# Linear attention into two mixture stages: the matmuls of an attention iteration in another order, and three buffers for the raw weights

## The chip, the cores and the metric

The program runs on one core of a Trainium2 chip. The metric is the device time of one execution in microseconds (us), lower being better; the kernel before took 762.11 us in the median of three runs (761.12 to 762.54). The core has a matrix engine (TensorE, PE in the rows, with PEld for its weight loads), VectorE (DVE), ScalarE (ACT), GpSimd (POOL) and SyncE (SP). Each works through its own instructions in order. SP issues nearly all DMAs, POOL the indirect ones.

## The reference

Three stages follow each other. The first is gated linear attention over 4 batches, 8 heads, 768 steps and head size 48; the second sends each of the 3072 tokens to the best of 8 experts; the third multiplies two projections elementwise and applies two more matrices, which come as 64-bit floats.

```python
f = 1 / (1 + exp(-f_logit))
for t in range(S):                                   # attention, per batch and head
    state = f[t][:, None] * state + outer(k[t], v[t])
    y[t] = q[t] @ state
x = y.transpose(0, 2, 1, 3).reshape(3072, 384)
...
logits = (x / (norm(x) + 1e-6)) @ (emb / (norm(emb) + 1e-6)).T / tau
e = argmax(logits, 1)                                # expert of each token
gate = softmax(logits)[range(N), e]
x = gate[:, None] * (relu(x @ w1[e]) @ w2[e])        # per token's expert
...
a, b = x @ g1, x @ g2                                # g1, g2, g3, go: 64-bit inputs
out = ((a * b) @ g3) @ go
```

## The kernel before

The kernel has three stretches. In the first, 24 units of attention (4 batches by 6 chunks of 128 steps, all heads of a chunk at once) go through a loop of 26 iterations, software-pipelined: iteration i works on unit i for one part, on unit i-1 for the next, and so on to i-4. The table `parts` (L685) sets the order of the parts, each with how many units it lags; every engine gets its instructions in that order, and the program's order is kept. In the second stretch each expert's tokens are fetched, multiplied by w1 and w2 (`g1_step`, L824, and `g2_step`, L838), and written to a dense buffer; in the third the two projections and the output follow (L921 and L934).

The parts of one iteration, with the tile that each writes: `s_gate` turns the gates of unit i (ft, L343) and makes their sigmoid on ACT (L351, L352); `s_qk` turns q and k of unit i-1 (qt, kt, L343) and scales them on DVE (qd and kd, L371 and L373); `s_scan` makes the running products on DVE (L357, L359); `s_score` multiplies kd by qd for unit i-2 (a, L382), and ACT and POOL copy and mask the result (am, L384 and L385); `s_kb` turns kd (kb, L394); `s_uu` makes the state's increment of unit i-3 from kk and v (uu, L424), which `s_state` adds on DVE (L433), `s_sm` scales on POOL (L440) and `s_blocks` copies on ACT (sbd, L448); `s_out` makes the outputs of unit i-3, first from the state (y, L405), then from am and v (y, L408); `s_xt` turns them to token rows and makes the logits (xl, L454), which ACT copies (xt, L455) and DVE sums (lg, L464). There are eight accumulator banks, given out in turn, so that a matmul also waits until the tile of eight allocations before has been read.

The matmuls use the 128 by 128 array in three ways. ft, qt, kt, kb, xl and the y of L405 use all rows and columns; a works on 64 rows at a time (64\*128 in the rows of the profile); uu and the y of L408 write 64 columns at a time (128\*64). Below, such a way is called an array mode.

Beside the attention, three things run in the loop. `route` (L494) ranks finished units by expert in groups of four: some 20 small DVE instructions, a power on POOL (L510), a few matmuls (rk) and one indirect DMA a unit (L556) that scatters its tokens to the scratch xsd. It is a generator; `turn` advances it by one step four times an iteration (twice that in the last two). `conversions` (L197) turns the 64-bit weights to 32 bits a piece at a time: a DMA of the raw piece (L207), two ACT instructions (L223, L224), two on DVE (L226, L227), one add on POOL (L230); `convert` and `bg.pull` advance it from iteration 5 on. In the first stretch it makes 16 pieces, in the second 20 more. At the end of an iteration SP loads the gates, k, q and v of later units (L333), the next raw piece and, in iterations 2 to 9, zeros for part of xsd (L718).

After the loop the last units are routed (`pre`, three units, and `last`, one), the counts of the experts are ranked (`finish_route`, L565), and the first expert's tokens are read back (xs, L783). PE fills this time with products of the two last matrices (wpb, L184).

Of the kernel before, what the change touches and what calls it, by code (L numbers as in the profile page):

```python
# [19 lines left out]
def attn_moe_glu_kernel(  # L20
# [21 lines left out]
    P = 128  # L42
# [65 lines left out]
    GAP_TILES, ZF, BG0, BGP = 4, 2, 5, 2  # L108
# [88 lines left out]
    def conversions(pieces):  # L197
        raws = {}

        def load_raw(i):  # L200
            if i < len(pieces):
                loads.append(lambda: fetch_raw(i))

        def fetch_raw(i):
            src, n, _, _ = pieces[i]
            raws[i] = cv.tile([P, 512, 2], I32, name="raw", bufs=2)[:, 0:n, :]
            SP.dma_start(out=raws[i], in_=src.bitcast(I32).rearrange("p (n w) -> p n w", w=2))  # L207

        load_raw(0)
        load_raw(1)  # L210
        for i, (_, n, tag, put) in enumerate(pieces):
# [164 lines left out]
    def s_score(u):  # L376
        qd, kd = st["qd", u], st["kd", u]
        m = wk.tile([P, 2, NP, P], F32, name="am")
        a = [bank([P, NP, P], "a") for _ in range(2)]
        for j in range(NP):  # L380
            for hb in range(2):
                PE.matmul(out=a[hb][:, j, :], lhsT=kd[64 * hb:64 * hb + 64, j, :], rhs=qd[64 * hb:64 * hb + 64, j, :])  # L382
        for hb in range(2):
# [14 lines left out]

    def s_out(u):
        b, c = units[u]  # L400
        am, qd = st.pop(("am", u)), st.pop(("qd", u))
        vv = vs[u % NV]
        y = bank([P, NP, P], "y")
        for j in range(NP if c else 0):
            PE.matmul(out=y[:, j, :], lhsT=sbd[b][:, j, :], rhs=qd[:, j, :], start=(j == 0), stop=False, skip_group_check=True)  # L405
# [64 lines left out]
    def make_en():  # L470
        et = rt.tile([E, DM], F32, name="et")
        s = rt.tile([E, 6], F32, name="es")
        ep = rt.tile([E, H, 64], F32, name="ep")
# [20 lines left out]
    def route(u0, n):  # L494
# [6 lines left out]
        t8 = lambda name: rt.tile([P, 4, E], F32, name=name, bufs=2)[:, 0:n, :]  # L501
        t1 = lambda name, dt=F32: rt.tile([P, 4], dt, name=name, bufs=2)[:, 0:n]
        mx, m2, m, d = t1("mx"), t1("m2"), t8("m"), t8("d")
        r0, r1, rinv = t1("r0"), t1("r1"), t1("rinv")
        nb = rt.tile([P, E], F32, name="nb", bufs=2)
        sq = ssq[:, us]
        t, sm = t8("t"), t1("sm")
        pos, pi = t1("pos"), rt.tile([P, 4], I32, name="pi", bufs=2)[:, 0:n]
        flat = lambda a: a.rearrange("p g e -> p (g e)")
        G.tensor_tensor(out=r0, in0=sq, in1=half[:, 0:1].to_broadcast([P, n]), op=ALU.pow)  # L510
# [4 lines left out]
        V.tensor_tensor(out=d, in0=L, in1=wide(mx), op=ALU.subtract)  # L515
# [12 lines left out]
        V.tensor_scalar(out=r1, in0=r1, scalar1=0.5, scalar2=1e-6, op0=ALU.mult, op1=ALU.add)  # L528
# [4 lines left out]
        PE.matmul(out=flat(rk), lhsT=tri, rhs=flat(O), start=True, stop=False, skip_group_check=True)  # L533
# [4 lines left out]
        V.reciprocal(out=rinv, in_=r1)  # L538
# [559 lines left out]
```

## Time and profile before

| | us |
|---|---|
| median of three runs | 762.11 |
| the profiled execution: its whole time | 760.98 |
| its span, first to last instruction | 759.3 |
| PE busy | 732.8 (97%) |
| DVE, ACT, POOL busy | 362.8, 355.7, 361.1 |

The span begins with the first instruction and ends with the last; the whole time of that execution has 1.7 us more around it. Matmuls are pipelined, so that a busy PE row can still hold gaps between starts: the starts of successive groups tell how long a group kept PE. PEclk is the share of TensorE's full clock that was granted. Unless a row says otherwise, times are us from the start of the span.

### The profile page before, as it was taken

How to read it: one execution, taken by the hardware profiler on the slowest of the kernel's cores; microseconds unless marked ns; L12 is line 12 of the kernel's file. 1: busy time of each engine (PE TensorE's matmuls, PEld its weight loads, DVE VectorE, ACT ScalarE, POOL GpSimd, SP SyncE). 2: the span in 40 equal slices, each digit the busy share in tenths (PEclk: the TensorE clock that was granted, in tenths of full speed). 3: DMA queues.
4: the chain of work that ended last, by engine and by line, in shares of the span. 5: the costliest groups of instructions: out<-in, count | busy, mean ns of one | idle time of the engine just before them, and what ended most of it. 6: DMA issues, size and time to landing. Idle time of an engine off the chain costs nothing.

```text
span 759.3 us, 12752 instructions
## 1 busy us (share of the span) xinstructions
PE 732.8 (97%) x4825; PEld 666.6 (88%) x4825; DVE 362.8 (48%) x716; ACT 355.7 (47%) x723; POOL 361.1 (48%) x412
## 2 busy tenths in 40 slices
PE   6999899999899998999999999999999999999996
PEld 6888788788799998999999998888888888888885
DVE  8888799995646544543542323232222322323222
ACT  5899687884555646645554542212112112121220
POOL 4567778886497766756555681221112202211102
PEclk9999999999999999999999999999999999999999
DMA  9999978822576797646433340010010100100101
GB/s 184 246 243 247 244 180 210 216 56 94 186 255 209 228 254 228 209 132 203 146 115 123 126 126 1 0 42 1 1 41 1 43 0 1 42 1 2 41 1 45
DMA packets 132653, 89.64 MB, mean 118 GB/s; under 512 B 106465, under 2 KB 114665, under 8 KB 132585
## 3 DMA queue, kind: packets, MB, share of 16 engines
q1 hardware_dynamic: 129513, 79.29, 38.3%
q0 software_dynamic: 3072, 9.46, 3.4%
q8 instruction: 40, 0.66, 0.4%
q14 instruction: 28, 0.23, 0.1%
HBM read 70.57 MB, written 18.17 MB: 117 GB/s over the span
## 4 chain that ended last, share of the span: by engine, by line
PE 68%; issue 10%; DVE 8%; DMA 5%; POOL 4%; ACT 3%; SPq 0%; POOLq 0%; DVEq 0%; ACTq 0%
PE acc L838 12%; PE hb L824 11%; PE pa L921 10%; PE pb L921 10%; PE ob L934 10%; DMA stg<-in_moe_w_dram 3%; PE wpb L184 2%; PE a L382 2%; PE y L408 2%; DVE sf L357 2%; PE xl L454 2%; DVE w L359 1%; PE ft L343 1%; POOL xsd L556 1%; PE y L405 1%
## 5 line engine op out<-in xcount | busy, mean ns | idle before, releaser
L133 POOL TENSOR_TENSOR wl<-stg,wh 128x384 fp32r<-128x384 f32 (+1 forms) x121 | 139.0, 1172 | 67.6 <-ACT wh L132 59.1
L924 DVE TENSOR_TENSOR a<-a,pb 128x512 f32<-128x512 f32 x48 | 33.0, 688 | 181.5 <-PE pb L921 175.7
L934 PE MATMUL ob<-wp,ab 128*128 128x384 f32 x576 | 108.2, 339 | 0.0
L838 PE MATMUL acc<-h,wh 128*128 128x448 f32 (+7 forms) x384 | 104.3, 351 | 3.1 <-ACT h L826 2.2
L934 PEld LDWEIGHTS ob<-wp,ab 128*128 128x128 f32 x576 | 102.3, 188 | 3.7
L824 PE MATMUL hb<-xT,wh 128*128 128x448 f32 (+7 forms) x384 | 102.6, 348 | 0.0
L827 DVE SCALAR_TENSOR_TENSOR h<-hb,h 128x448 fp32r<-128x448 f32 (+7 forms) x64 | 37.1, 580 | 111.6 <-ACT h L826 111.5
L921 PE MATMUL pa<-x,wh 128*128 128x512 f32 x288 | 90.2, 394 | 0.0
L921 PE MATMUL pb<-x,wh 128*128 128x512 f32 x288 | 89.9, 393 | 0.0
L941 POOL DMA_INDIRECT out_dram<-o,didx x24 | 23.2, 968 | 129.8 <-DVE o L940 126.4
L923 ACT COPY a<-pa 128x512 f32<-128x512 f32 x48 | 28.2, 587 | 120.6 <-PE pa L921 120.6
L132 ACT CAST wh<-stg 128x384 fp32r<-128x384 f32 (+1 forms) x124 | 64.4, 566 | 39.6 <-DMA stg<-in_moe_w_dram 34.6
L133 POOL TENSOR_TENSOR x<-xd,x 128x512 fp32r<-128x512 f32 x18 | 22.8, 1292 | 121.4 <-ACT x L132 121.4
L926 ACT CAST ab<-a 128x512 fp32r<-128x512 f32 x48 | 29.8, 621 | 104.8 <-DVE a L924 104.8
L838 PEld LDWEIGHTS acc<-h,wh 128*128 128x128 f32 x384 | 70.4, 188 | 6.6 <-ACT h L826 3.2
L824 PEld LDWEIGHTS hb<-xT,wh 128*128 128x128 f32 x384 | 70.8, 188 | 1.4
L824 PE MATMUL hb<-xT,wl 128*128 128x448 f32 (+7 forms) x192 | 66.7, 348 | 0.0
L838 PE MATMUL acc<-h,wl 128*128 128x448 f32 (+7 forms) x192 | 66.7, 347 | 0.0
L921 PEld LDWEIGHTS pb<-x,wh 128*128 128x128 f32 x288 | 54.2, 188 | 12.7
L385 POOL TENSOR_SCALAR_AFFINE_SELECT am<-am 128x512 f32<-128x512 f32 x48 | 51.7, 1098 | 23.1 <-ACT am L384 23.1
L921 PEld LDWEIGHTS pa<-x,wh 128*128 128x128 f32 x288 | 53.6, 188 | 9.2
L826 ACT ACTIVATE h<-hb 128x448 fp32r<-128x448 f32 (+7 forms) x64 | 32.5, 508 | 61.3 <-PE hb L824 61.0
(184 smaller groups left out, 1363.8 us busy)
## 6 DMA issues: line engine op xcount, KB each, us to landing
stg<-in_moe_w_dram SPq DMA_DIRECT2D x32, 768.0 KB, 5.1
raw<-in_moe_w_dram SPq DMA_DIRECT2D x28, 512.0 KB, 4.2
xsd<-wp SPq DMA_DIRECT2D x8, 675.5 KB, 5.8
xs<-xsd SPq DMA_DIRECT2D x8, 675.5 KB
f<-in_f_logit_dram SPq DMA_DIRECT2D x24, 192.0 KB, 3.9
k<-in_k_dram SPq DMA_DIRECT2D x24, 192.0 KB, 4.4
q<-in_q_dram SPq DMA_DIRECT2D x24, 192.0 KB, 4.6
v<-in_v_dram SPq DMA_DIRECT2D x24, 192.0 KB, 4.3
```

The lines of the kernel that those rows point to most:

```text
L132: A.copy(out=hi, in_=src)
L133: eng.tensor_tensor(out=lo, in0=src, in1=f32(hi), op=ALU.subtract)
L385: G.affine_select(out=m[:, hb], in_=m[:, hb], pattern=[[0, NP], [1, P]], compare_op=ALU.is_ge, fill=0.0, base=0, channel_multiplier=-1)
L824: PE.matmul(out=b, lhsT=w[x][:, kk, cs], rhs=xT[e][y][:, kk, :], start=(kk + n == 0), stop=(kk == KD - 1 and n == 2))
L826: A.activation(out=h[0], in_=b, func=AF.Relu)
L827: V.scalar_tensor_tensor(out=h[1], in0=b, scalar=0.0, in1=f32(h[0]), op0=ALU.max, op1=ALU.subtract)
L838: PE.matmul(out=acc[d], lhsT=w[x][:, s % 4, d * P:(d + 1) * P], rhs=hs[s][y], start=(s + n == 0), stop=(s == KF - 1 and n == 2))
L921: PE.matmul(out=b, lhsT=w[x][:, kk, cs], rhs=x2[n][y][:, kk, :], start=(kk + m == 0), stop=(kk == KD - 1 and m == 2))
L923: A.copy(out=t, in_=pa)
L924: V.tensor_tensor(out=t, in0=t, in1=pb, op=ALU.mult)
L926: A.copy(out=ab[s][0], in_=t)
L934: PE.matmul(out=oacc[t], lhsT=ab[s][x][:, t * P:(t + 1) * P], rhs=wp[:, y, s, :], start=(s + m == 0), stop=(s == KF - 1 and m == 2))
```

## The change

The parts of an iteration are put in another order, and two of them are cut in two: `s_score` keeps the matmuls and leaves the copies and masks to `s_mask`, and the product with the state moves from `s_out` to `s_inter`. The raw weights get three buffers; the tile z goes, and its values overwrite the low words in the raw tile. A raw buffer is thereby free after the add on POOL, no longer after the second DVE instruction, and the next load is asked for there. `route` takes groups of six, makes the square root's correction without the extra step, ranks with fewer and wider matmuls, writes the position as an integer at once, and copies the ids on POOL. The zeros are written in iterations 2, 3, 5, 6, 7, 9, 10 and 11. Two small tiles of the start reuse others.

```diff
-    GAP_TILES, ZF, BG0, BGP = 4, 2, 5, 2
+    GAP_TILES, BG0, BGP, RAW = 4, 5, 2, 3
+    FILL = (2, 3, 5, 6, 7, 9, 10, 11)
...
-            raws[i] = cv.tile([P, 512, 2], I32, name="raw", bufs=2)[:, 0:n, :]
+            raws[i] = cv.tile([P, 512, 2], I32, name="raw", bufs=RAW)[:, 0:n, :]
...
-            z = cv.tile([P, 512], I32, name="z", bufs=2)[:, 0:n]
+            z = lo
...
+            A.activation(out=p, in_=lo.bitcast(U32), func=AF.Copy, scale=2.0 ** -29)
             A.activation(out=f32(z), in_=f32(hi), func=AF.Copy, scale=2.0 ** -112)
-            A.activation(out=p, in_=lo.bitcast(U32), func=AF.Copy, scale=2.0 ** -29)
             yield
             V.tensor_scalar(out=z, in0=z, scalar1=3, scalar2=None, op0=ALU.logical_shift_left)
             V.scalar_tensor_tensor(out=z, in0=hi, scalar=-(1 << 31), in1=z, op0=ALU.bitwise_and, op1=ALU.bitwise_or)
-            load_raw(i + 2)
             yield
             G.tensor_tensor(out=p, in0=z, in1=p, op=ALU.add)
+            load_raw(i + RAW)
...
+    def s_inter(u):
+        b, c = units[u]
+        qd = st.pop(("qd", u))
+        y = st["y", u] = bank([P, NP, P], "y")
+        for j in range(NP if c else 0):
+            PE.matmul(out=y[:, j, :], lhsT=sbd[b][:, j, :], rhs=qd[:, j, :], start=(j == 0), stop=False, skip_group_check=True)
...
-        V.tensor_copy(out=xt[:, xs, DM + 1].bitcast(I32), in_=ids[:, us])
+        G.tensor_copy(out=xt[:, xs, DM + 1].bitcast(I32), in_=ids[:, us])
...
-        V.tensor_scalar(out=r0, in0=r0, scalar1=1e-30, scalar2=None, op0=ALU.max)
-        V.reciprocal(out=r1, in_=r0)
-        V.tensor_tensor(out=r1, in0=sq, in1=r1, op=ALU.mult)
-        V.tensor_tensor(out=r1, in0=r1, in1=r0, op=ALU.add)
-        V.tensor_scalar(out=r1, in0=r1, scalar1=0.5, scalar2=1e-6, op0=ALU.mult, op1=ALU.add)
+        V.tensor_scalar(out=r0, in0=r0, scalar1=1e-6, scalar2=None, op0=ALU.add)
...
-        for j in range(n):
-            PE.matmul(out=rk[:, j, :], lhsT=ones, rhs=base, start=False, stop=False, skip_group_check=True)
-            for i in range(j):
-                PE.matmul(out=rk[:, j, :], lhsT=ones, rhs=O[:, i, :], start=False, stop=False, skip_group_check=True)
+        PE.matmul(out=rk, lhsT=ones, rhs=base.unsqueeze(1).to_broadcast(big), start=False, stop=(n == 1), skip_group_check=True)
+        for i in range(n - 1):
+            PE.matmul(
+                out=rk[:, i + 1:, :], lhsT=ones, rhs=O[:, i:i + 1, :].to_broadcast([P, n - 1 - i, E]),
...
-        V.tensor_reduce(out=pos, in_=t, axis=AX.X, op=ALU.add)
-        V.tensor_copy(out=pi, in_=pos)
+            V.tensor_reduce(out=pi, in_=t, axis=AX.X, op=ALU.add)
...
-    groups = {u0 + n - 1: (u0, n) for u0, n in ((0, 4), (4, 4), (8, 4), (12, 4), (16, 4))}
+    groups = {u0 + n - 1: (u0, n) for u0, n in ((0, 6), (6, 6), (12, 6), (18, 2))}
...
-            (s_state, 4), (s_gate, 0), (s_sm, 1), (s_qk, 1), (turn, None),
-            (s_scan, 0), (s_score, 2), (s_blocks, 1), (s_xt, 4), (turn, None), (s_x, 0),
-            (convert, None), (turn, None), (s_uu, 3), (turn, None), (s_lg, 4), (s_kb, 2),
-            (s_sq, 4), (convert, None), (s_out, 3),
+            (s_state, 4), (s_score, 2), (s_gate, 0), (s_qk, 1), (s_mask, 2), (turn, None),
+            (s_kb, 2), (s_sm, 1), (s_xt, 4), (s_blocks, 2), (s_scan, 0), (turn, None), (s_x, 0),
+            (s_inter, 3), (convert, None), (turn, None), (s_lg, 4), (s_sq, 4), (turn, None),
+            (s_out, 3), (s_uu, 3), (convert, None),
```

On PE, an iteration of the loop stood so before (the tiles are those of the section above, the numbers behind them buffers):

```order
L343 MATMUL ft<-ident,f_114 128x128 x4
L343 MATMUL qt<-ident,q_110 128x128 x4
L343 MATMUL kt<-ident,k_113 128x128 x4
L382 MATMUL a<-qd,kd 128x128 x8
L454 MATMUL xl<-sel,yT 128x104 x4
L424 MATMUL uu<-v_117,kk 64x48 x8
L394 MATMUL kb<-ident,kd 128x128 x4
L405 MATMUL y<-qd,sbd_121 128x128 x4
L408 MATMUL y<-am,v_117 64x128 x8
```

and stands so now, at the same place of the loop:

```order
L382 MATMUL a<-qd,kd 128x128 x8
L344 MATMUL ft<-ident,f_114 128x128 x4
L344 MATMUL qt<-ident,q_110 128x128 x4
L344 MATMUL kt<-ident,k_113 128x128 x4
L398 MATMUL kb<-ident,kd 128x128 x4
L462 MATMUL xl<-sel,yT 128x104 x4
L408 MATMUL y<-qd,sbd_124 128x128 x4
L416 MATMUL y<-am,v_120 64x128 x8
L432 MATMUL uu<-v_120,kk 64x48 x8
```

The scores moved to the front, and the state's increment to the end behind the outputs, so that the array mode changes three times an iteration instead of six: from uu to the next a, from a to ft, and from y (L408) to y (L416). Line numbers of the changed kernel are 1 to 8 higher than those of the kernel before.

On POOL, from the last mask of the loop to the last scatter, the order before was (r0 is the power of `route`, pi the positions of one group):

```order
L385 AFFINE_SELECT am_2625<-am_2625 128x512 x2
L556 DMA xsd_80<-xt_135,pi_2548 24576x386
L563 MEMSET half_71 128x1
...
L510 TENSOR_TENSOR r0_2740<-ssq_66,half_71 128x3
...
L510 TENSOR_TENSOR r0_2809<-ssq_66,half_71 128x1
L556 DMA xsd_80<-xt_135,pi_2747 24576x386
...
L556 DMA xsd_80<-xt_135,pi_2816 24576x386
```

and is now:

```order
L389 AFFINE_SELECT am_2521<-am_2521 128x512 x2
L561 DMA xsd_80<-xt_135,pi_2271 24576x386
L568 MEMSET half_71 128x1
...
L561 DMA xsd_80<-xt_135,pi_2441 24576x386
...
L517 TENSOR_TENSOR r0_2632<-ssq_66,half_71 128x3
L519 COPY xt_135<-ids_70 128x3
L517 TENSOR_TENSOR r0_2688<-ssq_66,half_71 128x1
L519 COPY xt_135<-ids_70 128x1
L561 DMA xsd_80<-xt_135,pi_2637 24576x386
```

Before, two scatters stood between the last mask and the power of `pre` (128x3), two more between it and the power of `last` (128x1), and four behind. Now eight stand ahead of the power of `pre` (six with the positions pi_2271, two with pi_2441), none between the two powers, and four behind.

On SP, a raw load waits now for POOL's add of the piece three before it, where it waited for DVE's second instruction of the piece two before it; its place behind the loads of an iteration is the same.

## Rows read from the trace of the kernel before

**Rows 1.** The busy time of each engine in five stretches: iterations 4 to 6, 7 to 13, iteration 14, iterations 15 to 23, and all from the first expert on. The columns: start and end of the stretch, its length, then busy time and count of instructions of PE, PEld, DVE, ACT and POOL, then PEclk, the DMA share and GB/s.

```profile
20.73:38.23 17.50, 17.50 (x219) 15.15 (x217) 15.26 (x25) 14.41 (x30) 9.15 (x13) 1.00 1.02 240
38.23:85.70 47.47, 47.41 (x574) 42.27 (x572) 38.89 (x87) 39.31 (x89) 34.14 (x41) 1.00 0.97 244
85.70:97.75 12.05, 9.27 (x91) 8.08 (x92) 9.30 (x14) 9.01 (x20) 10.46 (x13) 0.86 1.07 251
97.75:164.47 66.72, 62.05 (x720) 54.64 (x718) 64.59 (x131) 55.09 (x122) 54.84 (x65) 1.00 0.72 175
...
203.52:759.30 555.78, 545.10 (x2805) 500.02 (x2804) 191.21 (x291) 205.94 (x401) 218.61 (x211) 1.00 0.29 89
```

**Rows 2.** Timeline of PE over one iteration without a wait: start, length, engine, line, operation, tiles, shape (rows\*columns of the array), count of instructions (two for a matmul that is not a transpose).

```profile
105.46 0.66 PE L343 MATMUL ft<-ident,f 128*128 128x128 f32 x4
105.95 0.60 PE L343 MATMUL qt<-ident,q 128*128 128x128 f32 x4
106.39 0.60 PE L343 MATMUL kt<-ident,k 128*128 128x128 f32 x4
106.92 1.16 PE L382 MATMUL a<-qd,kd 64*128 64x128 f32 x16
108.01 1.14 PE L454 MATMUL xl<-sel,yT 128*128 128x104 f32 x8
109.08 0.67 PE L424 MATMUL uu<-v,kk 128*64 128x48 f32 x16
109.68 0.66 PE L394 MATMUL kb<-ident,kd 128*128 128x128 f32 x4
110.18 1.06 PE L405 MATMUL y<-qd,sbd 128*128 128x128 f32 x8
111.16 1.09 PE L408 MATMUL y<-am,v 128*64 128x128 f32 x16
112.19 0.66 PE L343 MATMUL ft<-ident,f 128*128 128x128 f32 x4
```

**Rows 3.** Timeline of ACT in iteration 13, with the idle time before an instruction and what ended it.

```profile
84.16 0.55 ACT L223 ACTIVATE z<-raw 128x384 f32<-128x384 f32 x1 [2.57 <-DMA raw<-in_moe_w_out_dram]
```

**Rows 4.** Timeline of SP, the issue of the raw piece for which ACT waited there.

```profile
79.11 0.56 SPq L207 DMA_DIRECT2D raw<-in_moe_w_out_dram  x1
```

**Rows 5.** Timeline of all engines in iteration 14.

```profile
86.43 1.23 DVE L357 TENSOR_TENSOR_SCAN sf<-fg,downs 128x516 f32<-128x516 f32 x1 [3.11 <-ACT fg L352]
...
90.65 1.99 PE L382 MATMUL a<-qd,kd 64*128 64x128 f32 x14 [2.65 <-DVE lg L464]
...
92.56 1.90 PE L454 MATMUL xl<-sel,yT 128*128 128x104 f32 x8
```

**Rows 6.** Groups of DVE instructions in iterations 15 to 23, by line: count, then busy us and mean ns of one. Of the 22 groups of `route` (lines 511 to 552, 49 instructions, 16.7 us together) the largest and the smallest are here, and two of one size (L524 and L518).

```profile
L542 DVE TENSOR_TENSOR base<-nb,base 128x8 bf16<-128x8 f32 x3 | 2.2, 719 | 0.0
L524 DVE TENSOR_TENSOR oh<-m,m 128x32 bf16<-128x32 f32 x2 | 2.1, 1059 | 0.0
...
L518 DVE TENSOR_TENSOR m<-m,wrev 128x32 f32<-128x32 f32 x2 | 0.4, 180 | 0.0
...
L516 DVE TENSOR_SCALAR r<-r 128x4 f32<-128x4 f32 x2 | 0.3, 157 | 0.0
```

**Rows 7.** What PE waited for in iterations 15 to 23: us in total, times, longest.

```profile
PE a L382 <- DVE lg L464: 2.6, 4, 1.2
PE xl L454 <- DVE scm L433: 1.4, 1, 1.4
```

**Rows 8.** Timeline of POOL at the end of the attention.

```profile
174.66 1.23 POOL L385 TENSOR_SCALAR_AFFINE_SELECT am<-am 128x512 f32<-128x512 f32 x2
177.00 0.98 POOL L556 DMA_INDIRECT xsd<-xt,pi  x1 [1.11 <-DVE lg L464]
...
178.28 0.96 POOL L556 DMA_INDIRECT xsd<-xt,pi  x1 [0.18 <-issue]
...
179.30 0.90 POOL L510 TENSOR_TENSOR r<-ssq,half 128x3 f32<-128x3 f32 x1
...
190.37 0.96 POOL L556 DMA_INDIRECT xsd<-xt,pi  x1 [0.19 <-DVE slot_r L600]
```

**Rows 9.** Timeline of DVE there.

```profile
180.23 0.17 DVE L516 TENSOR_SCALAR r<-r 128x3 f32<-128x3 f32 x1 [1.61 <-POOL r L510]
...
184.01 0.19 DVE L464 TENSOR_REDUCE lg<-xl 128x8 f32<-128x32 f32 x1 [2.40 <-ACT xt L455]
...
189.98 0.17 DVE L600 TENSOR_SCALAR slot_r<-sl 128x8 int32<-128x8 f32 x1
```

**Rows 10.** Timeline of PE there: the last scores, and the first expert's tokens.

```profile
170.62 1.16 PE L382 MATMUL a<-qd,kd 64*128 64x128 f32 x16
...
199.90 1.68 PE L811 MATMUL xb<-ident,xs 112*128 112x112 f32 x12 [1.74 <-ACT xs L802]
```

**Rows 11.** What SP waited for from 203 to 460 us: us in total, times, longest.

```profile
SPq L207 <- DVE z L227: 72.1, 17, 11.9
SPq L139 <- POOL gt L230: 11.5, 12, 1.1
```

**Rows 12.** What PE waited for from 203.52 us to the end.

```profile
PE acc L838 <- ACT h L826: 2.2, 3, 1.4
PE acc L838 <- DVE h L827: 0.9, 4, 0.4
```

More of the change, by code (lines that the diff above doesn't have):

```diff
@@ L377, in s_score @@
         qd, kd = st["qd", u], st["kd", u]
-        m = wk.tile([P, 2, NP, P], F32, name="am")
-        a = [bank([P, NP, P], "a") for _ in range(2)]
+        a = st["a", u] = [bank([P, NP, P], "a") for _ in range(2)]
         for j in range(NP):
@@ L382, in s_score, with s_mask @@
                 PE.matmul(out=a[hb][:, j, :], lhsT=kd[64 * hb:64 * hb + 64, j, :], rhs=qd[64 * hb:64 * hb + 64, j, :])
+    def s_mask(u):
+        a = st.pop(("a", u))
+        m = wk.tile([P, 2, NP, P], F32, name="am")
         for hb in range(2):
@@ L397, in s_kb @@
         st["kk", u] = kk
+    def s_inter(u):
[4 more added lines that the diff above has]
+            PE.matmul(out=y[:, j, :], lhsT=sbd[b][:, j, :], rhs=qd[:, j, :], start=(j == 0), stop=False, skip_group_check=True)
     def s_out(u):
         b, c = units[u]
-        am, qd = st.pop(("am", u)), st.pop(("qd", u))
+        am, y = st.pop(("am", u)), st.pop(("y", u))
         vv = vs[u % NV]
-        y = bank([P, NP, P], "y")
-        for j in range(NP if c else 0):
-            PE.matmul(out=y[:, j, :], lhsT=sbd[b][:, j, :], rhs=qd[:, j, :], start=(j == 0), stop=False, skip_group_check=True)
         for j in range(NP):
@@ L470, in make_en @@
     def make_en():
-        et = rt.tile([E, DM], F32, name="et")
+        et = wk.tile([P, 2, NP, P], F32, name="am")[0:E].rearrange("e a b d -> e (a b d)")[:, 0:DM]
         s = rt.tile([E, 6], F32, name="es")
-        ep = rt.tile([E, H, 64], F32, name="ep")
+        ep = wk.tile([P, NP, P], F32, name="yT")[0:E].rearrange("e a (b d) -> e (a b) d", b=2)
         SP.dma_start(out=et, in_=emb)
@@ L532, in route @@
         rk = bank(big, "rk")
-        PE.matmul(out=flat(rk), lhsT=tri, rhs=flat(O), start=True, stop=False, skip_group_check=True)
-        for j in range(n):
-            PE.matmul(out=rk[:, j, :], lhsT=ones, rhs=base, start=False, stop=False, skip_group_check=True)
-            for i in range(j):
-                PE.matmul(out=rk[:, j, :], lhsT=ones, rhs=O[:, i, :], start=False, stop=False, skip_group_check=True)
-        V.reciprocal(out=rinv, in_=r1)
+        PE.matmul(out=rk, lhsT=tri, rhs=O, start=True, stop=False, skip_group_check=True)
+        PE.matmul(out=rk, lhsT=ones, rhs=base.unsqueeze(1).to_broadcast(big), start=False, stop=(n == 1), skip_group_check=True)
+        for i in range(n - 1):
+            PE.matmul(
+                out=rk[:, i + 1:, :], lhsT=ones, rhs=O[:, i:i + 1, :].to_broadcast([P, n - 1 - i, E]),
+                start=False, stop=(i == n - 2), skip_group_check=True,
+            )
+        V.tensor_tensor(out=d, in0=L, in1=wide(mx), op=ALU.subtract)
+        V.reciprocal(out=rinv, in_=r0)
         yield
@@ L544, in route @@
         A.activation(out=d, in_=d, func=AF.Exp)
-        V.tensor_reduce(out=pos, in_=t, axis=AX.X, op=ALU.add)
+        with nc.allow_low_precision(reason="one term of the sum is a whole number, the others are 0"):
+            V.tensor_reduce(out=pi, in_=t, axis=AX.X, op=ALU.add)
         yield
-        V.tensor_copy(out=pi, in_=pos)
         V.tensor_reduce(out=sm, in_=d, axis=AX.X, op=ALU.add)
@@ L716, in attn_moe_glu_kernel @@
                 SP.dma_start(out=idd.rearrange("(p c) w -> p (c w)", c=32), in_=zero[0:DENSE // 32, 0, 0:32].bitcast(I32))
-            if ZF <= i < ZF + E:
-                SP.dma_start(out=xsd[(i - ZF) * N:(i - ZF) * N + CAP, :].rearrange("(p c) w -> p c w", c=4), in_=zero[0:CAP // 4])
+            if i in FILL:
+                e = FILL.index(i)
+                SP.dma_start(out=xsd[e * N:e * N + CAP, :].rearrange("(p c) w -> p c w", c=4), in_=zero[0:CAP // 4])
             if i >= BG0:
@@ L729, in attn_moe_glu_kernel @@
         step(times_w[0])
+        s_inter(NU - 1)
         s_out(NU - 1)
-        s_uu(NU - 1)
         s_lg(NU - 2)
```

16 lines of the change are left out of this document (7 added, 9 removed).

## The prediction

> **What bounds the kernel now.** I read the page first, for the share of each engine by slice: PE is busy 97% of the span, and it is full in nearly every slice behind the attention. So a gain there would need shorter matmuls, and the change has none; what it can win lies in the first 200 us, and what it wins there ought to pass to the end as it is. Next comes the table of stretches [rows 1]. It shows four regimes of the loop. In iterations 4 to 6 and 7 to 13 PE is full (47.41 of 47.47 us in the second), with ACT and DVE at 39 us: PE sets the pace, at 6.73 us an iteration (from ft at 105.46 to ft at 112.19, a later iteration without a wait [rows 2]). Iteration 14 alone takes 12.05 us. In iterations 15 to 23 DVE is busy 64.59 of 66.72 us while PE is busy 62.05 and waits 2.6 us for DVE's lg and 1.4 for its scm [rows 7]: DVE sets the pace there, PE is close behind it.
>
> The timeline of PE shows what the array mode costs [rows 2]. Four turns last 0.44 us from start to start where the same mode stands on both sides (qt to kt). Behind a change they take 0.49 (ft), ahead of one 0.53 (kt): 0.05 to enter, 0.09 to leave. The eight y of L405 take 0.98 with a change behind them, so 0.89 without; the eight xl, of nearly the same length, take 1.07 between two changes, 0.18 more. kb takes 0.50, 0.06 to enter. That y starts on time behind kb tells that a new tile by itself costs nothing.
>
> Iteration 14 is a stall with a cause in SP's queue: the raw piece was issued at 79.11 [rows 4], ACT stood 2.57 us for it until 84.16 [rows 3], DVE 3.11 for ACT, PE 2.65 for DVE, and then 14 instructions of a took 1.99 us and eight of xl 1.90 where 16 and eight take 1.16 and 1.14 [rows 2, 5]. The granted clock over this stretch is 0.86 [rows 1]: after PE had stood idle, part of it ran at 1.2 GHz instead of 2.4.
>
> **The change part by part.** *Order of the matmuls.* Of six changes of mode three go. In the full-array groups that removes kt's leaving (0.09), xl's two (0.18) and kb's entering (0.06), 0.33 us. uu's entering and y's leaving go too; no row shows these two without a change, so they are worth 0 to 0.09 each, and I take 0.06 as for kb: 0.45 an iteration, between 0.33 and 0.51. Three iterations give 1.35, seven give 3.15. For iterations 24 and 25, one change each, 0.15: 0.3. That assumes no cost between y and uu, which now stand side by side with another length but one mode. The Trainium skill (TensorEngine Tiling (Array Packing), Key Properties) says that a change of mode, not of the tile alone, drains the array; the full-array rows agree at 0.05 to 0.09 a side. By its rule y to uu is free, as I have it; if it drained like the others, 0.15 of the 0.45 would come back, 1.5 us over ten iterations, and no row here shows that pair.
>
> At 6.28 us an iteration ACT, 39.31 us in seven iterations, would be 89% busy [rows 1]; iterations 15 to 23 ran with DVE at 97%, so ACT should hold. It has less slack than before in one place: uu now takes the bank of this iteration's a, so PE's last group waits for ACT's copies am, which stand behind the two of ft. I cost this at nothing, because PE reaches uu some 4 us after a.
>
> *Three raw buffers.* A load is issued a whole piece earlier than before, against a wait for POOL instead of DVE. The piece at 84.16, issued at 79.11, is then issued when the piece before the last one is done, an estimated 5 us or more earlier, so ACT finds it landed. Then iteration 14 costs what its neighbours cost, 6.3: 5.75 of its 12.05 us go, the lost clock with them. Bounds: nothing (another wait steps in), 5.8. SP, behind the raw load, holds the next gates, k, q and v; these are used three iterations after their issue, so some microseconds of waiting cost nothing there. In the second stretch the same wait stands ahead of the experts' weights, for which ACT and then PE wait a little now: all of PE's waits from 203.52 us on are 3.1 us [rows 12]. SP stood 72.1 us for raw pieces there already [rows 11]. I take 0, between 3.1 saved and the rival below.
>
> *z in the raw tile.* The same instructions run on every second word instead of neighbours. No row shows DVE's shift on such a tile; the second DVE instruction already reads one. From 0 to 0.2 us a piece, on engines that wait; 0.
>
> *Route.* Groups of six and fewer steps take DVE from 49 route instructions in iterations 15 to 23 to 21 (counted in its order between the first scans of iterations 14 and 23). The 49 are 16.7 us [rows 6], so 28 are 9.5. DVE would fall from 64.59 to about 56, under PE's 62.05 - 9 x 0.45 = 58.0. So PE is late next, and 58.0 with the same share of waits as now (66.72 / 64.59) is 59.9: 6.8 us go. Bounds: 3.0 (below) and 8.7 (PE without a wait). POOL's six small copies of ids and the wider rk matmuls are hidden under PE.
>
> *The end of the attention.* Here the change adds. Before, the last scatter started 19.75 us behind the last scores (190.37 - 170.62) [rows 8, 10], and DVE had the slot of the first expert's tokens at 189.98, 6.0 us behind the last lg [rows 9]. Now POOL has eight scatters between the last mask and the power of `pre`, where it had two. The mask can start 1.7 us behind the scores, since no scatters stand ahead of it, and takes 1.23 [rows 8]; eight scatters at 1.28 apart (177.00 to 178.28) end 13.2 us behind the scores, the power (0.90) at 14.1. DVE's correction of r0 waits for that, and behind it in DVE's queue stands the whole last routing and ranking. Before it went on at 180.23, 9.6 us behind the scores [rows 9], but then waited for the last lg until 13.4. So the chain starts some 1.1 us later and is six small instructions shorter (0.5); the four last scatters also start about 1 us later. PE only waits there (1.74 us now [rows 10]). I take 1.0 us lost, between -0.5 and 4 (scatters that take 1.9 instead of 1.28).
>
> The sum: 1.35 + 3.15 + 0.3 + 5.75 + 6.8 - 1.0 = 16.35. The profiled execution took 760.98 us, 1.1 under the median: 744.6, and **745.8 us** beside the median of 762.11.
>
> **The rivals.** *The late stretch keeps its waits.* Of the same size, oh takes 1059 ns and m 180 [rows 6]: much of route's time on DVE is waiting for something, and that something is POOL, busy 54.84 us there [rows 1]. If these waits move to the scans and the conversions, the 28 instructions give back only their own 0.18 us, less the 0.08 by which DVE's instructions overlap (the groups of that view add up to 74.6 us, 131 instructions, over 64.59 busy): 2.8 us. DVE stays at 61.8, the stretch at 63.8, and 3.0 go instead of 6.8: 749.6 us. The Trainium skill (SBUF — State Buffer, Who interferes with whom) has the rule: a DVE instruction with two SBUF inputs and a GpSimd instruction that reads SBUF shut each other out for a whole instruction. Its mechanism is this rival.
>
> *The stall only moves.* Nothing guarantees that a loop at 6.3 us finds every buffer in time: SP's loads share the DMA engines, whose share is 0.97 to 1.07 up to iteration 14 [rows 1]. One stall like that of iteration 14 takes its 5.75 back: 751.6.
>
> *Slower: raw loads hold SP in the second stretch.* A raw load waits there for POOL's add, and the add comes behind the weights' splits in POOL's queue; scratch stores waited up to 1.1 us for the same adds even after DVE's part was done [rows 11]. The experts' weights stand behind the raw load. When they came late, PE lost up to 1.4 us at a time [rows 12]. With 20 pieces there, each costing PE 1.4, 28 us are lost: 773.8. From twelve such pieces on the kernel is slower. Against it: the raw loads wait 72.1 us there now and PE loses 3.1 in all.
>
> *It does not do what it says.* If a change of mode cost nothing and the gaps came from the tiles, 4.8 us of the sum would go and the late stretch would stay at PE's 62.05, 3 us more: 753.6. The start of y behind kb speaks against it.
>
> **How the numbers follow.** The forecast has a chance of 0.55, the late waits 0.17, the moved stall 0.12, no effect of the modes 0.04, the held SP 0.07; 0.05 is for what I do not see. About 0.2%, 1.5 us, is what a measurement can tell from no change. The first four are all faster by over that: 0.88 with a little of the rest dropped. Slower is the held SP from twelve pieces on and part of the unseen: 0.08; the same, 0.04. The low end adds the unpriced gains to the forecast: 3.1 us of waits behind the attention, 1.9 of the late stretch, 0.6 of the modes and some of the end: 739. The high end takes late waits and a moved stall together, 755.4, and a slow end: 757. Left out below and above is about 0.2.
>
> **What would show it.** Right: ft starts 6.2 to 6.4 us apart in iterations 7 to 13; no wait of ACT for a raw piece; iterations 15 to 23 at 6.5 to 6.8 us with PE and DVE close to each other; the first hb some 15 to 17 us earlier than 203.52, and from there to the end 555.8 us as now. Wrong: a stretch with a granted clock under 1.00 inside the loop; PE waiting for am at uu; affine masks or scans longer than now in the late stretch; more than 20 us from the last scores to the last scatter; waits of PE for h that add up to more than 3.1 us.

## The result, and the profile after

The changed kernel took 770.48 us (median; 770.02 to 771.04), the kernel before 762.33 beside it: a ratio of 1.0109, interval 1.0091 to 1.0126. It is 1.1% slower where 2.1% faster was forecast. The span of the profiled execution grew by 9.6 us, from 759.3 to 768.9. Taken apart at the places that the prediction spoke of (starts of ft, the first hb, the first pa of the third stretch):

| stretch | before | after | change | forecast |
|---|---|---|---|---|
| to iteration 4 | 20.73 | 22.52 | +1.8 | 0 |
| iterations 4 to 6 | 17.50 | 16.01 | -1.5 | -1.35 |
| iterations 7 to 13 | 47.47 | 45.81 | -1.7 | -3.15 |
| iteration 14 | 12.05 | 6.25 | -5.8 | -5.75 |
| iterations 15 to 23 | 66.72 | 68.81 | +2.1 | -6.8 |
| from there to the first hb | 39.05 | 44.06 | +5.0 | +0.7 |
| experts | 246.19 | 255.63 | +9.4 | 0 |
| behind | 309.59 | 309.81 | +0.2 | 0 |

The scores now stand ahead of ft in an iteration: 1.1 us of the first row is this shift of the mark, and the sixth row is 1.1 too small for it. So the start lost 0.7 us and the end 6.1.

The busy time of each engine in these stretches after the change (columns as in [rows 1]):

```profile
22.52:38.53 16.01, 16.01 (x219) 15.18 (x217) 14.39 (x25) 13.05 (x29) 9.66 (x10) 1.00 1.03 232
38.53:84.34 45.81, 44.37 (x570) 41.98 (x568) 41.05 (x74) 42.07 (x96) 36.96 (x43) 1.00 0.99 252
84.34:90.59 6.25, 6.25 (x83) 5.95 (x81) 4.78 (x10) 4.73 (x11) 4.55 (x4) 1.00 1.00 221
90.59:159.40 68.81, 60.31 (x705) 55.51 (x703) 66.86 (x102) 56.43 (x122) 59.47 (x78) 0.95 0.79 194
203.46:459.09 255.63, 247.49 (x1366) 238.93 (x1365) 111.39 (x170) 140.42 (x286) 167.01 (x143) 0.99 0.55 172
```

In the fourth row DVE has 29 instructions fewer than in [rows 1] and is busy 2.3 us longer, POOL 4.6 longer. The groups of that stretch (columns as in [rows 6]), first after, then the lines of before that answer to them:

```profile
L358 DVE TENSOR_TENSOR_SCAN sf<-fg,downs 128x516 f32<-128x516 f32 x9 | 17.3, 1928 | 0.0
L561 POOL DMA_INDIRECT xsd<-xt,pi x12 | 14.4, 1196 | 2.1 <-issue 1.7 <-DVE qd L372 0.2 <-DVE scm L441 0.2
L527 DVE TENSOR_TENSOR oh<-m,m 128x48 bf16<-128x48 f32 x2 | 4.6, 2300 | 0.0
L374 DVE TENSOR_TENSOR kd<-kt,sf 128x512 f32<-128x512 f32 x9 | 6.1, 679 | 0.0
```

```profile
L357 DVE TENSOR_TENSOR_SCAN sf<-fg,downs 128x516 f32<-128x516 f32 x9 | 14.2, 1574 | 0.1
L556 POOL DMA_INDIRECT xsd<-xt,pi x8 | 10.2, 1269 | 1.4 <-issue 1.2 <-DVE xt L512 0.2
```

The scan takes 0.35 us longer each time, and the groups of six have put twelve scatters into the stretch where eight were. Two iterations hold the loss: iteration 18 took 10.53 us (8.68 before) and iteration 23 9.29 (6.45); the other seven won 2.6 together. What DVE's lateness does to PE is seen in iteration 18 (timeline of PE): PE stands 2.27 us for lg, and then eight xl take 1.87 us where they took 1.14 [rows 2], since the clock is down to half (0.50 granted from 117.60 to 119.47).

```profile
116.95 0.85 PE L398 MATMUL kb<-ident,kd 128*128 128x128 f32 x4 [2.27 <-DVE lg L472]
117.60 1.87 PE L462 MATMUL xl<-sel,yT 128*128 128x104 f32 x8
```

The end of the attention, timelines of POOL, DVE, SP and PE after, and what SP waited for there:

```profile
179.04 0.90 POOL L517 TENSOR_TENSOR r<-ssq,half 128x3 f32<-128x3 f32 x1
...
186.74 0.96 POOL L561 DMA_INDIRECT xsd<-xt,pi  x1 [0.19 <-DVE flag L612]
...
179.98 0.19 DVE L530 TENSOR_SCALAR r<-r 128x3 f32<-128x3 f32 x1 [5.92 <-POOL r L517]
...
187.01 0.40 SPq L266 DMA_DIRECT2D stg<-in_moe_w_dram  x1
192.84 0.35 SPq L789 DMA_DIRECT2D xs<-xsd  x1
...
198.23 2.24 PE L817 MATMUL xb<-ident,xs 112*128 112x112 f32 x12 [3.92 <-ACT xs L808]
200.15 3.47 PE L185 MATMUL wpb<-wo,w3t 128*128 128x384 f32 x12
...
SPq L789 <- DMA xsd<-xt,pi: 4.5, 1, 4.5
```

The last scatter starts 20.9 us behind the last scores (186.74 - 165.82), as forecast within 0.2. But xs leaves 6.1 us behind it, where it left 3.7 behind before (194.09 - 190.37). Between them stands a weight load (stg) that SP issued 0.3 us behind the scatter. The scatter landed late: it took 5.9 us from issue to landing, the longest of the last scatters, where the last one of before took 3.5. The rows, which cover those whose landing the trace has, after and then before:

```profile
DMA to landing us min/median/max: 2.7/4.3/5.9
```

```profile
DMA to landing us min/median/max: 3.5/3.5/3.5
```

PE then idles 3.92 us instead of 1.74 [rows 10], and twelve wpb run partly at half clock (3.47 us against 2.33 before; 0.63 granted from 200.15 to 203.46).

In the experts' stretch, what SP and PE waited for (before: [rows 11, 12]), and one such wait followed through POOL, SP, ACT and PE:

```profile
SPq L266 <- POOL wl L134: 84.4, 21, 9.4
SPq L208 <- POOL gt L230: 45.7, 11, 6.4
SPq L208 <- ACT raw L225: 37.9, 8, 10.6
SPq L208 <- POOL g L230: 14.7, 5, 4.8
...
PE acc L844 <- ACT h L832: 6.7, 5, 2.6
PE acc L844 <- DVE h L833: 1.4, 7, 0.4
```

```profile
264.28 1.32 POOL L230 TENSOR_TENSOR gt<-raw,gt 128x512 int32<-128x512 int32 x1 [1.15 <-PE xb L817]
...
265.62 0.33 SPq L208 DMA_DIRECT2D raw<-in_moe_w_dram  x1
...
267.28 0.39 SPq L266 DMA_DIRECT2D stg<-in_moe_w_dram  x1
...
275.60 0.62 ACT L133 CAST wh<-stg 128x512 fp32r<-128x512 f32 x1 [6.18 <-DMA stg<-in_moe_w_dram]
...
276.68 0.46 PE L844 MATMUL acc<-h,wh 128*128 128x416 f32 x1 [2.62 <-ACT h L832]
```

SP stands for raw pieces 98.3 us (45.7 + 37.9 + 14.7) instead of 72.1. POOL's add ends at 265.6; only then the raw load goes, and the weights behind it, issued at 267.28, come 6.18 us late for ACT, whose cast stands ahead of h. Before, with the first hb at the same time, the raw load at this place of SP's queue went at 260.01 and the weights behind it at 262.55. PE's waits are 8.1 us instead of 3.1; the rest of the 9.4 is half clock behind them (PE busy 247.49 instead of 243.07, mean clock 0.99).

### The profile page after: what moved, and what is told of

Its sections match the earlier page's. It is cut to its first block, busy times and chain, and to the rows that moved or that the text cites. A ratio compares the mean times of both kernels' runs of the same rounds, so it can differ in the third digit from the quotient of the medians.

```text
span 768.9 us, 12645 instructions
## 1 busy us (share of the span) xinstructions
PE 728.6 (95%) x4791; PEld 668.8 (87%) x4791; DVE 363.9 (47%) x658; ACT 356.4 (46%) x722; POOL 363.2 (47%) x417
## 4 chain that ended last, share of the span: by engine, by line
PE 64%; issue 11%; DVE 9%; DMA 7%; ACT 4%; POOL 4%; SPq 0%; POOLq 0%; ACTq 0%; DVEq 0%
PE acc L844 10%; PE pa L927 10%; PE pb L927 10%; PE hb L830 10%; PE ob L940 10%; DMA stg<-in_moe_w_dram 6%; PE wpb L185 3%; PE a L382 2%; DVE sf L358 2%; PE y L416 1%; PE xl L462 1%; DVE w L360 1%; PE ft L344 1%; POOL xsd L561 1%; PE y L408 1%
## 5 line engine op out<-in xcount | busy, mean ns | idle before, releaser
L844 PE MATMUL acc<-h,wh 128*128 128x448 f32 (+7 forms) x384 | 106.5, 356 | 8.1 <-ACT h L832 6.7
L833 DVE SCALAR_TENSOR_TENSOR h<-hb,h 128x448 fp32r<-128x448 f32 (+7 forms) x64 | 37.1, 579 | 118.0 <-ACT h L832 117.9
L830 PE MATMUL hb<-xT,wl 128*128 128x448 f32 (+7 forms) x192 | 67.3, 350 | 0.0
```

Source lines behind the costliest of these rows:

```text
L830: PE.matmul(out=b, lhsT=w[x][:, kk, cs], rhs=xT[e][y][:, kk, :], start=(kk + n == 0), stop=(kk == KD - 1 and n == 2))
L833: V.scalar_tensor_tensor(out=h[1], in0=b, scalar=0.0, in1=f32(h[0]), op0=ALU.max, op1=ALU.subtract)
L844: PE.matmul(out=acc[d], lhsT=w[x][:, s % 4, d * P:(d + 1) * P], rhs=hs[s][y], start=(s + n == 0), stop=(s == KF - 1 and n == 2))
```

## The experiments

They ran on other chips of the kind, each beside the kernel before, whose runs there spread from 758 to 768 us (one of 1437 left out); so single stretches of the traces say more than the totals. A trace is of one execution: those of raw_undone and raw_alone were the slowest of their kernels, 3.2 and 2.6 us above the median, that of route_undone the fastest, 4.7 below. Two traces of one kernel differ by up to 1.5 us in the late stretch (after 68.8 and 67.3, before 66.7 and 65.4). Where an expectation gives 66.5 us for the late stretch of the kernel after, it was counted to 7 us behind the last ft; counted to the first qt of iteration 24, as here and in [rows 1], it is 68.8.

**The kernels unchanged.**

> The kernel after, unchanged, beside runs of the kernel before on the same chip. In three of the four runs so far ACT stood 2 to 6 us in the end of the attention for something that the trace names only as remote, and the first trace of the kernel after has no such wait. Theory: the wait is of this chip's runs and of the line of eight scatters, so that it shows here too, with the first hb at 206 to 212 and a time of 772 to 778. Rival, it came from the edits: no such wait, first hb at 203 to 204, time 769 to 772.

768.77 us, 1.0106 (1.0063 to 1.0148), the rival nearly: no such wait of ACT, the first hb at 202.47. The experts took 254.0, the late stretch 67.3.

> The kernel before, unchanged, for its trace on this chip. Both theories take it to be as in the first trace: the stall of 10 to 13 us in iteration 13 or 14, 65 to 68 us for the nine iterations behind it, 32 to 35 us from the last scores to the first hb, 245 to 247 in the experts; no wait of ACT for something remote. If it has that wait too, the line of eight scatters is not its cause.

762.28 us, 0.9987 (0.9970 to 1.0004). Iteration 14 took 13.3 us, the late stretch 65.4, the way from the last scores to the first hb 32.6, the experts 246.19. ACT had no such wait, but DVE stood 2.4 us in the end of the attention for something that the trace names only as remote.

**One part undone.** The raw pieces as before:

```diff
-GAP_TILES, BG0, BGP, RAW = 4, 5, 2, 3
+GAP_TILES, BG0, BGP, RAW = 4, 5, 2, 2
-            z = lo
+            z = cv.tile([P, 512], I32, name="z", bufs=2)[:, 0:n]
...
+            load_raw(i + RAW)
             yield
             G.tensor_tensor(out=p, in0=z, in1=p, op=ALU.add)
-            load_raw(i + RAW)
```

> The kernel after, with the raw pieces as before: two buffers, z in its own tile, the next load behind DVE's second instruction. Theory: the raw loads' wait for POOL holds SP in the experts' stretch, so that stretch falls from 255.6 us back to 246 to 247.5; the stall of one iteration in the loop may come back (0 to 5.8). Total 761 to 767. Rival, the stretch is longer for another reason (its first expert starts badly): it stays at 254 to 256 and the total is 770 to 776.

767.94 us, 1.0066 (1.0032 to 1.0099). The experts fell to 244.7, even below the range: the theory held. ACT stood 6.23 us for a raw piece again and iteration 13 took 12.3: the buffers are what took this wait away. The total stayed 0.9 above the range; in the trace iteration 18 took 13.6, and ACT stood 6.3 us at the end for something remote.

The order of the parts as before (the table of the diff reversed, s_mask behind s_score, s_inter ahead of s_out):

> The kernel after, with the parts of an iteration in the order of before. Theory: iterations 4 to 6 go back to 5.8 us and those behind to 6.7, about 4.8 us lost by iteration 14, the late stretch stays at 64 to 67 us; total 773 to 776. Rival, the new order is what sets POOL's masks beside DVE's scans: the late stretch falls to 59 to 62 us, and the total comes out at 767 to 771.

774.85 us, 1.0166 (1.0104 to 1.0228). Iterations 4 to 6 took 17.50 and iteration 4 began at 20.71: what is lost at the start belongs to the order. The late stretch took 67.9, so the rival fell. The total came out in the range, but iteration 17 took 13.2 and ACT stood 4.1 us at the end for something remote, neither of which was expected.

The route as before (its steps and groups of four):

> The kernel after, with route as before (its steps and its groups of four). Theory: DVE's time in the late stretch is mostly waiting for POOL, so that 28 more instructions cost 2 to 4 us there (66.5 becomes 68.5 to 70.5), the end of the attention is about 1 us shorter, the total 771 to 774. Rival, the new route is what lengthens the scans: the late stretch falls below 65, and the total to 766 to 769.

776.82 us, 1.0196 (1.0145 to 1.0246), slower than either expected. Iteration 13 took 15.7 us; the reason is found with groups_of_four, and it makes the total useless for route's worth. The late stretch went the way of the rival, if not so far: 65.9 us instead of 68.8, with DVE less busy for 29 instructions more, and with shorter scans (the stretch, and its scan):

```profile
102.54:168.48 65.94, 58.04 (x720) 53.06 (x719) 64.28 (x131) 56.54 (x123) 54.59 (x66) 1.00 0.73 175
```

```profile
L358 DVE TENSOR_TENSOR_SCAN sf<-fg,downs 128x516 f32<-128x516 f32 x9 | 14.7, 1629 | 0.0
```

**One part alone, in the kernel before.** Three raw buffers and z in the raw tile (those lines of the diff):

> The kernel before with the three raw buffers and z in the raw tile alone. Theory: iteration 14 costs about 6.9 instead of 12.05 (5 to 6 us won in the loop), and the experts' stretch takes 254 to 256 instead of 246.2 (8 to 10 lost); total 2 to 5 us above the kernel before. Rival, the weights are late because of the new order or route: the stretch stays at 246 to 247 and the total falls by 5.

770.42 us, 1.0100 (1.0067 to 1.0133): this part alone makes the kernel slower. The experts took 254.6, PE waited 7.4 us for h. Iteration 14 fell to 7.0, but iteration 15 took 12.2 without ACT waiting for a raw piece, and so the total is above the range.

The order of the parts alone (s_mask, s_inter and the table):

> The kernel before with the new order of the parts alone. Theory: 0.48 us less in each iteration without a wait (5.34 and 6.25), 1 to 2 us lost in iteration 1, the stall for the raw piece still there (10 to 13 us in one or two iterations), the late stretch as before at 64 to 68, the experts at 245 to 247; total 0 to 5 us below the kernel before. Rival, the new order sets POOL's masks beside the scans: the late stretch takes 70 or more and the total is above the kernel before.

760.07 us, 0.9961 (0.9941 to 0.9980), as the theory had it: 16.01 in iterations 4 to 6, iteration 13 at 11.8, the late stretch 66.8, the experts 243.7 (1.3 below the range).

The route alone (its function and groups 6, 6, 6, 2):

> The kernel before with the new route and its groups of six alone. Theory: the late stretch is 2 to 4 us shorter than 66.7, the end of the attention from the last scores to the first hb is longer than 32.9 by 2 to 8 (eight scatters in line, the last behind the first weights), the experts stay at 246; total 0 to 5 us above the kernel before. Rival, its 28 instructions fewer on DVE are worth what was forecast: the late stretch falls by 6 and the total by 3 to 6.

764.45 us, 1.0037 (1.0012 to 1.0063), as the theory had it, with less won in the loop: the late stretch 65.9, of which iteration 17 took 12.2; from the last scores to the first hb 37.1; xs left 6.3 us behind the last scatter. The three parts alone add up to +1.0%, the change to +1.1%. That is in part luck: each of the three still has an iteration of about 12 us, and the kernel after has none over 10.5.

**The tokens ahead of the weights.**

```diff
-        step(ahead)
         xs_load(0)
         step(ahead)
+        step(ahead)
```

> The kernel after, with the load of the first expert's tokens asked for ahead of the first load of expert weights on SP. Theory: the last scatter lost its place in the DMA engines to that weight load (issued 186.74, its packets moved at 191.3 to 192.1, behind the weights at 188.1 to 191.7). Then the tokens' load leaves at about 190.5 instead of 192.84, the first hb starts at 200 to 201.5 instead of 203.46, and the time is 2 to 3.5 us below that of the kernel after. Rival, the line of twelve scatters is what is late: the tokens' load stays at 192 to 193 and the time within 0.5 us of the kernel after, or above it, since the weights then come later.

776.63 us, 1.0203 (1.0149 to 1.0257): worse. xs did leave 2.9 us behind the last scatter, not 6.1, so the weight load had held up the scatter; but the weights now came late, ACT cast them before it touched the tokens, and the first hb stood at 209.1. The rival's last words were right. This trace also has a wait that the one of the kernel after hasn't, and its last scatter started 24.4 us behind the last scores, not 20.9, so that the total isn't the price of the edit alone (timeline of ACT, in the middle of eight scatters on POOL):

```profile
179.89 0.58 ACT L421 COPY yT<-y 128x512 f32<-128x512 f32 x1 [6.23 <-remote]
```

**The raw loads of the second stretch behind the weights.**

```diff
-                issue()
+                held, loads[:] = loads[:], []
                 bg.pull(3)
...
                     step(ahead)
+                for f in held:
+                    f()
```

> The kernel after, with each raw load of the experts' stretch asked for one step later and behind the expert weights of that step on SP. Theory: there the raw load, waiting for POOL's add, stood ahead of the weights in SP's queue; behind them it holds nobody. The stretch falls from 254.0 to 255.6 us to 244 to 247, PE's waits for h from 6.6 us to under 2.5, the time to 758 to 762. Rival, it is z in the raw tile (the longer hold of ACT, DVE and POOL on a piece) and not the place in the queue: the stretch stays above 251 and the time above 766.

759.23 us, 0.9956 (0.9934 to 0.9978). The experts took 241.67, less than in either kernel, though z still lies in the raw tile. What is left of PE's waits there, and the stretch:

```profile
PE acc L844 <- DVE h L833: 0.4, 1, 0.4
```

```profile
205.84:447.51 241.67, 241.24 (x1366) 236.63 (x1365) 100.69 (x170) 141.08 (x286) 166.89 (x143) 1.00 0.57 182
```

So it was the place in SP's queue, behind the weights and so a step later. Five of the six kernels below have this edit, all but the one without masks, and 241.6 to 241.9 there.

**The groups.** On top of loads_later:

```diff
-((0, 6), (6, 6), (12, 6), (18, 2))
+((0, 6), (6, 6), (12, 4), (16, 4))
```

> As loads_later, with route's groups 6, 6, 4, 4 instead of 6, 6, 6, 2, so that four scatters of the third group go out inside the loop. Theory: fewer scatters stand ahead of the power of the last groups; DVE's wait for it (5.9 us in the kernel after) falls below 3, the last scatter starts 19 to 20 us behind the last scores instead of 20.9; 1 to 2 us less than loads_later. Rival, the four scatters come back as waits of DVE in the late stretch: the time is the same as loads_later or 1 to 3 above.

754.44 us, 0.9896 (0.9869 to 0.9922). DVE no longer waits for the power, the last scatter starts 20.6 behind the last scores, the first hb 34.1 (40.8 in loads_later, where ACT stood 6.2 us as above). More was won than the scatters explain; most of it is that wait.

Loads_later with the route as before:

> As loads_later, with route as before (groups of four). Theory: route's 28 instructions fewer gave little, since their time on DVE was waiting; the loop is 3 to 8 us longer than in loads_later, the way from the last scores to the first hb 2 to 4 shorter; the time 1 us below to 5 above loads_later. Rival, the new route costs by itself: 3 us or more below loads_later.

764.94 us, 1.0031 (1.0010 to 1.0053): 5.7 us above loads_later, a little more than the theory's most, and iteration 13 took 16.1 (7.3 in loads_later), which is more than the whole difference. The late stretch took 66.2 where loads_later has 69.0: without the wait of iteration 13 the rival would have been nearer. Groups of four throughout, with the new steps:

> As groups_6644, with groups of four throughout and the new steps of route. Theory: what the groups cost or save in the loop is within 2 us, and what counts is the line of scatters at the end, which is the same as in groups_6644: no wait of ACT for something remote there, last scatter 19 to 21 us behind the last scores, time 752 to 757. Rival, the groups of six are worth their fewer instructions: 2 to 4 us above groups_6644.

765.73 us, 1.0036 (1.0012 to 1.0059), far outside. The end was as expected (no wait of ACT, 19.2 us), but iteration 13 took 18.0. Its trace shows why (SP and POOL):

```profile
80.78 0.43 SPq L724 DMA_DIRECT2D xsd<-wp  x1
...
86.89 1.21 POOL L561 DMA_INDIRECT xsd<-xt,pi  x1 [10.05 <-DMA f<-in_f_logit_dram]
```

The first scatter of a group of four comes in iteration 13 and waits for the last zeros, which the change writes in iteration 11. The row names f, which is inferred; the zeros could be tried:

```diff
-    FILL = (2, 3, 5, 6, 7, 9, 10, 11)
+    FILL = (2, 3, 4, 5, 6, 7, 8, 9)
```

> As groups_of_four, with the zeros for the scatter's rows written in iterations 2 to 9 as in the kernel before. There the first scatter (POOL, 86.89) stood 10.05 us for the last zeros, which had been asked for at 80.78, and the whole loop with it: iteration 13 took 18.0 us. Theory: the later zeros and the groups of six belong together; with the zeros early again the first scatter waits for nothing, iterations 13 and 14 take 6.3 to 8 us each, the time falls from 765.7 to 752 to 757, beside groups_6644. Rival, the groups of four cost by their own scatters and instructions: the time stays above 760.

757.90 us, 0.9935 (0.9914 to 0.9955), 0.9 above the range. The first scatter starts at 78.3 without a wait and iteration 13 takes 7.3; iteration 14 still takes 10.8 (PE 1.82 us for am). The late stretch took 66.9. The later zeros and the groups of six belong together; the three kernels that took one of them back measured that.

**The late stretch.** The kernel after without the affine masks:

```diff
-            G.affine_select(out=m[:, hb], in_=m[:, hb], ...)
```

> The kernel after without the affine masks of the scores on POOL (the part above the diagonal stays in, so the outputs are others). Theory: DVE's scans in the late stretch are long because POOL's masks and DVE keep each other waiting: eight L358 scans, 15.8 us there, fall to 10 to 12 us, DVE's busy time per iteration by 0.5 or more, and the late stretch from 66.5 to 58 to 62 us. Rival, the scans wait for something else (the conversions' adds, the scatters' descriptors): L358 stays at 15 or more and the stretch at 64 to 67.

769.89 us in one run. The stretch fell to 63.36, DVE's busy time in it by 13.3 us to 53.58 with the same 102 instructions, the scan to 1368 ns:

```profile
89.60:152.96 63.36, 58.57 (x705) 54.16 (x703) 53.58 (x102) 55.59 (x122) 41.48 (x55) 0.97 0.91 221
```

```profile
L358 DVE TENSOR_TENSOR_SCAN sf<-fg,downs 128x516 f32<-128x516 f32 x9 | 12.3, 1368 | 3.9 <-ACT fg L353 3.9
```

A fifth of DVE's time there was waiting that POOL's masks caused. The total gained nothing: ACT stood 8.2 us at the end for something remote, and the experts took 253.1. Masks kept but moved ahead of the gates, on top of groups_6644:

```diff
-(s_score, 2), (s_gate, 0), (s_qk, 1), (s_mask, 2), (turn, None),
+(s_score, 2), (s_mask, 2), (s_gate, 0), (s_qk, 1), (turn, None),
```

> As groups_6644, with the copies and masks of the scores put ahead of the gates in an iteration, so that POOL's masks fall beside DVE's qd and kd, which no mask has lengthened, and no longer beside its scans. Theory: the nine iterations from 15 on take 60 to 64 us instead of 67.4, the first scan's eight instances 11 to 13 us instead of 16.7, the time 3 to 6 us below groups_6644. Rival, the scans now start later (ACT makes the gates behind the copies) and DVE idles for it: the stretch stays at 66 to 69, the time within 1 us or above.

753.04 us, 0.9858 (0.9835 to 0.9880), the fastest of all, 1.4% below the kernel before. But its stretch is 68.35 beside 69.20, less than two traces of one kernel differ by, and its scan 2011 ns beside 2190: the rival, nearly. POOL is busy 57 of these 68 us, and a mask that leaves the scan falls beside another instruction of DVE. With groups_6644 the intervals overlap.

## Why the prediction was wrong

*Order of the matmuls: right.* 0.45 us was forecast, 5.83 to 5.34 and 6.73 to 6.25 are 0.49 and 0.48. Start to start in the iteration from 44.78, kt takes 0.43 (0.53), xl 0.87 (1.07), kb 0.44 (0.50), y of L416 0.92 (1.03), uu 0.56 (0.60), with before in brackets; y to uu has no cost, as the Trainium skill's rule (TensorEngine Tiling (Array Packing), Key Properties) had it. Iterations 12 and 13 lost 1.0 each, where PE came to wait for DVE's scm and lg: the slack that the text looked for in ACT ended in DVE. And the start was not looked at: with the scores in front, PE stands in iterations 2 and 3 for kd (1.04 and 0.51 us).

*Three raw buffers: right in the loop, wrong behind it.* The stall for the raw piece went as forecast. With the order of before one iteration still took 12 to 13 us with the three buffers (15 in raw_alone, 17 in order_undone), without ACT waiting for a raw piece, so the rival of a moved stall had its case too. The step that failed is "I take 0, between 3.1 saved and the rival below". The rival that was given 0.07 is what happened; its mechanism was right, its price too high: 9.4 us over 20 pieces is 0.47 a piece, not 1.4. The argument against it, that the 72.1 us of waiting cost PE only 3.1, proved nothing: those waits ended mostly in time, and the new ones end later (the raw load that went at 245.2 before has its like at the same place of the queue at 249.4, with the first hb at the same time). Two runs show the cause: with the release as before the experts took 244.7, and with the late raw loads moved behind the weights 241.7. A queue that waits without harm has slack, and the slack has to be read off, not assumed.

*Route: the step that failed is "6.8 us go".* It priced 28 instructions by their durations, of which about half were waits (an estimate: the 49 took 16.7 us, and at the 0.18 of the short ones [rows 6] they would take 8.8), and left POOL's own part out: four more scatters in the stretch, 4.2 us. The first rival saw that the waits would move to the scans and still let the instructions' own time be won. Not even that came: the stretch is 2.1 us longer. With the new order the new route costs 2.8 to 2.9 us there, as 65.9 (route_undone) beside 68.8 and 66.2 (route_old_loads_later) beside 69.0 show; both have the long iteration 13 ahead, which may have its part. The new steps with groups of four took 66.9 (fours_early_zeros), which points to the groups of six and their twelve scatters more than to the steps. In the order of before the new route took 65.9 beside 66.7 and 65.4: no clear gain either.

By the Trainium skill (SBUF — State Buffer, Who interferes with whom) a DVE instruction with two SBUF inputs shuts out, and is shut out by, a GpSimd one that reads SBUF. The rows agree: the scan, with two such inputs, went from 1928 to 1368 ns when the masks were left out, kd, with one input from the accumulators, stayed at 679 and 680.

*The end of the attention: the term was right, and the list was short.* "I take 1.0 us lost" measured 1.2. Not seen were the scatter held up by the weight load (2.4), half clock behind PE's longer idling (1.6, less 0.4 by which the tokens came sooner behind their load), and 1.3 in iterations 24 and 25, where PE waits 1.15 for lg.

*The balance.* Of the 17 us that the forecast summed up as gains, 9.0 came; 18.3 were lost at four places: the start (0.7), the late stretch (2.1), the end (6.1) and the experts (9.4). Four of the five signs that the prediction named for being wrong came: a granted clock under 1.00 in the loop (0.95 in the late stretch), longer scans, 20.9 us from the last scores to the last scatter, and waits for h of 8.1 us. PE never waited for am at uu.

## What to carry to other kernels

When a buffer's release moves to a later engine, read the queue that waits for it: what stands behind the waiting load is what gets late, and moving that load behind the urgent ones in the same queue may win more than the buffer. Durations on an engine that a busy neighbour holds up contain waits; here 28 instructions fewer on DVE gave back nothing, with POOL busy 59 of 69 us. Before one part of a change is undone as a test, look for another part that is tuned to it, as the zeros were to the groups.

## What the runs showed of the hardware

A load issued close behind a scatter can hold it up. In the kernel after, with the first weights issued 0.3 us behind POOL's last scatter, xs left 6.1 us behind the scatter; with xs asked for ahead of the weights (tokens_first) it left 2.9 behind. Seventeen traces have xs behind the weights. In three the weights went 0.2 to 0.4 us behind the start of the scatter (after, route_alone, no_mask), and xs 6.1 to 6.4; in thirteen the weights went 0.75 to 1.9 behind, and xs 3.2 to 3.9. One stands apart (order_undone: 1.1 and 5.8), so the gap between the two issues doesn't decide alone. In the trace of the kernel after, the scatter's packets move at 191.3 to 192.1, when nearly all of the weights' have gone (188.0 to 191.7). The Trainium skill (DMA: Bandwidth & Descriptors, Queues, rings and completion order) says that each DMA engine takes turns between queues packet by packet. By that rule a scatter that was ready would have shared; here it shared only the last 0.4 us, and whether its packets were ready before, the trace doesn't show.

ACT's wait for something that the trace names only as remote (2.0 to 8.2 us) showed in five of the eight traces with six or eight scatters in a line, in none of the ten without; but in one of those ten DVE had such a wait (before_again, 2.4 us). The five ran on two chips. Six traces without the line ran on the same two, without that wait of ACT, so the chip alone doesn't bring it about; two traces with the line ran on a third chip, also without it. What ACT and DVE wait for stays open.
